# The first half tile of a fused attention-memory and MoE kernel as a fixed script with plain 32-bit products

## The chip, the cores and the metric

The kernel runs on one core of one Trainium2 chip. The metric is the device time of one execution in microseconds (us). TensorE (PE) does the matrix products, VectorE (DVE) and ScalarE (ACT) the work on elements, GpSimd (POOL) and SyncE (SP) mostly issue transfers (DMA).

## What is computed

Four batches of eight heads with 576 tokens each go through an attention on a small memory; its output, 2304 tokens of 512, goes through two layers with 2048 hidden features.

```python
a = exp(phi - max(phi, axis=2)); a = a / (sum(a, axis=2) + 1e-9)     # 4 x 8 x 576 x 32, over the tokens
k_m = einsum('bhsm,bhsd->bhmd', a, k); v_m = einsum('bhsm,bhsd->bhmd', a, v)
scores = q @ k_m.T / sqrt(64)                                        # 576 x 32 for each head
attn = softmax(scores)                                               # over the 32 memory rows
x = attn @ v_m                                                       # 2304 x 512
x = square(relu(x @ w_in1)) @ w_out1                                 # layer 1
h = x @ w_in2; x = (h * tanh(softplus(h))) @ w_out2                  # layer 2
```

The weights arrive as 64-bit floats, which the kernel reads as pairs of 32-bit words and turns into 32-bit floats itself.

## The kernel before

**Tiles.** Layer 1 works on half tiles (b, half) of T = 288 tokens. The features are taken in groups of 4, 6 and 6 chunks of 128 (`GROUPS`); for each group the loop over `subs` runs through (0,0), (0,1), (1,0) and (1,1), and batches 2 and 3 follow later. The attention's last product is not made on its own: `w_part` (L474) and `w_turn` (L488) multiply v_m with W_in1 into `wp`, and a chunk's `h` is `wp` times the attention weights `a_t`. `a_tile` (L567) does one half tile: for each chunk six products for `h` (L580 to L582), relu (L589), square (L590), a high part `g` on ACT (L594) and the low part on DVE (L597); three chunks later (LAG = 3) `mm2_step` (L536) adds twelve products into four accumulators `a` (L542 to L544). Each product of two 32-bit matrices is written as three products of high and low parts (high by high, low by high, high by low).

**Weights.** `Conv` (L147), called c1, loads raw weights of 512 KB and converts 32 of them for layer 1: a Prelu on ACT (L185), a shift (L207) and a shift with "or" (L214) on DVE, and for W_out1 a high cast on ACT (L180) and a low part on DVE (L222). Each chunk calls `tick` (L168) once, and `c1.limit` says up to which conversion it may start. `win` are the converted pages of W_in1, which L218 also writes back to memory (`w_i`) for later use; `ct_o` and `o1h`, `o1l` are those of W_out1. A raw buffer that comes free lets SP issue the next load (L164).

**Attention.** For batch b `kv_soft` (L349) takes the maximum and exponential of phi, `kv_turn` (L359) transposes them (`pt`, `et`), `kv_mem` (L382) makes k_m and v_m (`pk`, `kk`), `kv_heads` (L405) turns those into `kT` and `vT` by way of `pkt`. `attn_unit` (L433) computes the scores of one half tile (`psc`, L439), their softmax on DVE and ACT, the transposed weights `at` (L462), and their high and low parts `ah` (L468) and `al` (L469). It is a generator in four steps; the lists `lanes` hand such steps out, one or three for each chunk.

**Order.** The pools and the tile framework decide the order of the instructions on an engine by their data and by `behind(...)`, which makes an instruction wait for a mark; `ahead` (L346) places products of h behind pieces of batch 1's memory and scores. Eight products of the identity with itself (`warm`, L629) run ahead of everything. All loads go through one queue on SP; they land in the order of issue.

## Time and profile before

| | us |
|---|---|
| median of 3 runs | 753.77 (751.84 to 756.18) |
| the profiled execution | 753.87 |
| its span on the core | 752.1 |
| PE busy | 722.5 |
| DVE busy | 527.0 |
| ACT busy | 420.3 |

The page counts for each engine the time in which it executed something; a share is an average over stretches with different limits. An idle time stands with the instruction that follows it, with the engine that released that instruction. The granted clock of PE is either full (1.00) or half (0.50).

### The profile page before, as it was taken

The numbers are of one execution on the slowest core, as the hardware profiler recorded it, in microseconds if no ns is written. First come the engines' busy times: TensorE is split into PE (matmuls) and PEld (weight loads), VectorE is DVE, ScalarE is ACT, GpSimd is POOL, SyncE is SP. The second block draws the span as 40 slices with busy tenths as digits, with TensorE's granted clock in tenths as the row PEclk, the third lists the DMA queues.
The fourth block names the chain that finished last, engine by engine and source line by source line (L and its number), as shares of the span: only waits on it lengthen the run. The fifth ranks groups of instructions, "written<-read, shape, count | busy, mean of one in ns | idle before, by whom it ended". The sixth has DMA issues, their size and how long they took to land.

```text
span 752.1 us, 16243 instructions
## 1 busy us (share of the span) xinstructions
PE 722.5 (96%) x5984; PEld 695.1 (92%) x5984; DVE 527.0 (70%) x1129; ACT 420.3 (56%) x960; POOL 62.3 (8%) x120
## 2 busy tenths in 40 slices
PE   5699999999998999989999999999999999999998
PEld 4487899999887989889999999999999999999998
...
PEclk9699999999999999999999999999999999999999
...
GB/s 334 405 407 73 202 189 144 182 240 359 316 338 273 172 249 305 266 280 261 343 39 322 259 267 352 244 302 263 323 267 255 248 285 278 256 236 270 245 266 73
DMA packets 89327, 195.33 MB, mean 260 GB/s; under 512 B 9888, under 2 KB 22688, under 8 KB 89248
## 3 DMA queue, kind: packets, MB, share of 16 engines
...
q10 hardware_dynamic: 144, 0.13, 0.1%
...
## 4 chain that ended last, share of the span: by engine, by line
PE 77%; DMA 6%; issue 6%; ACT 5%; DVE 3%; POOL 2%; SPq 0%; POOLq 0%; ACTq 0%
PE hb L979 8%; PE hb L981 8%; PE hb L980 8%; PE a L542 6%; PE a L544 6%; PE a L543 6%; PE h L580 3%; PE h L582 3%; PE h L581 3%; DMA raw_i<-in_moe_w_in_dram 2%; POOL wf_o L302 2%; DMA kv<-in_kvm_dram 1%; DMA wf_o<-st 1%; PE pk L397 1%; DMA wf_i<-st 1%
## 5 line engine op out<-in xcount | busy, mean ns | idle before, releaser
L542 PE MATMUL a<-g,o1h 128*128 128x288 f32 x512 | 147.9, 299 | 3.8 <-DVE g L596 1.1
L543 PE MATMUL a<-g,o1l 128*128 128x288 f32 x512 | 147.1, 297 | 0.0
L544 PE MATMUL a<-g,o1h 128*128 128x288 f32 x512 | 127.0, 296 | 0.8 <-DVE g L597 0.5
L979 PE MATMUL hb<-ych,u 128*128 128x384 f32 x336 | 112.9, 336 | 0.1
L980 PE MATMUL hb<-ycl,u 128*128 128x384 f32 x336 | 113.0, 336 | 0.0
L1024 DVE TENSOR_TENSOR opl<-a,oph 128x384 fp32r<-128x384 f32 x144 | 79.1, 557 | 46.9 <-ACT oph L1023 46.3
L981 PE MATMUL hb<-ych,u 128*128 128x384 f32 x336 | 109.5, 336 | 0.0
L1023 ACT CAST oph<-a 128x384 fp32r<-128x384 f32 x144 | 73.9, 513 | 58.8 <-PE b20b L1047 7.0
L542 PEld LDWEIGHTS a<-g,o1h 128*128 128x128 f32 x512 | 96.3, 189 | 7.0 <-ACT g L594 2.8
L543 PEld LDWEIGHTS a<-g,o1l 128*128 128x128 f32 x512 | 96.6, 189 | 0.0
L985 ACT ACTIVATE a<-hs 128x384 f32<-128x384 f32 x72 | 37.8, 525 | 98.1 <-DVE hs L989 98.0
L544 PEld LDWEIGHTS a<-g,o1h 128*128 128x128 f32 x512 | 88.5, 190 | 2.7 <-DVE g L597 1.9
L580 PE MATMUL h<-ah,wp 128*128 128x288 f32 x256 | 79.2, 311 | 6.8 <-ACT wp L485 2.7
L589 ACT ACTIVATE s<-h 128x288 f32<-128x288 f32 x128 | 52.3, 410 | 56.1 <-PE h L582 53.9
L582 PE MATMUL h<-ah,wp 128*128 128x288 f32 x256 | 76.4, 300 | 0.7 <-DVE wp L486 0.7
L581 PE MATMUL h<-al,wp 128*128 128x288 f32 x256 | 76.4, 299 | 0.0
L597 DVE TENSOR_TENSOR g<-s,g 128x288 fp32r<-128x288 f32 x128 | 57.0, 451 | 17.9 <-ACT g L594 16.8
L989 DVE TENSOR_TENSOR hs<-hu,hb 128x384 f32<-128x384 f32 x72 | 39.8, 554 | 40.7 <-PE hb L981 40.1
L979 PEld LDWEIGHTS hb<-ych,u 128*128 128x128 f32 x336 | 63.0, 188 | 0.4 <-DMA u<-wf_i 0.4
L980 PEld LDWEIGHTS hb<-ycl,u 128*128 128x128 f32 x336 | 63.0, 188 | 0.0
L981 PEld LDWEIGHTS hb<-ych,u 128*128 128x128 f32 x336 | 62.8, 188 | 0.0
L580 PEld LDWEIGHTS h<-ah,wp 128*128 128x128 f32 x256 | 48.5, 190 | 15.4 <-ACT wp L485 3.6
...
## 6 DMA issues: line engine op xcount, KB each, us to landing
u<-wf_i SPq DMA_DIRECT2D x168, 256.0 KB, 3.7
u<-wf_o SPq DMA_DIRECT2D x168, 256.0 KB, 3.4
raw_i<-in_moe_w_in_dram SPq DMA_DIRECT2D x32, 512.0 KB, 6.1
raw_o<-in_moe_w_out_dram SPq DMA_DIRECT2D x32, 512.0 KB, 6.0
wf_o<-st POOLq DMA_DIRECT2D x56, 256.0 KB, 4.9
wf_i<-st POOLq DMA_DIRECT2D x44, 256.0 KB, 4.5
win1r<-w_i SPq DMA_DIRECT2D x16, 512.0 KB, 6.8
...
```

The source lines that it names most:

```text
L542: nc.tensor.matmul(o, wh[:, c, cs], sh, start=first, stop=False)
L543: nc.tensor.matmul(o, wl[:, c, cs], sh, start=False, stop=False)
L544: done_pe["main"] = nc.tensor.matmul(o, wh[:, c, cs], sl, start=False, stop=last)
L580: nc.tensor.matmul(ph, w[:, 0, hg, fs], hi[:, hg], start=(hg == 0), stop=False)
L581: nc.tensor.matmul(ph, w[:, 0, hg, fs], lo[:, hg], start=False, stop=False)
L582: done_pe["h"] = nc.tensor.matmul(ph, w[:, 1, hg, fs], hi[:, hg], start=False, stop=(hg == 1))
L597: marks["low"] = nc.vector.tensor_sub(sl, s, sh.bitcast(F32))
L979: nc.tensor.matmul(ps, wh, yh[:, d], start=(j < 4 and d == 0), stop=False, **kw)
L980: nc.tensor.matmul(ps, wh, yl[:, d], start=False, stop=False, **kw)
L981: nc.tensor.matmul(ps, wl, yh[:, d], start=False, stop=end, **kw)
L1023: marks["s"] = nc.scalar.copy(hi, x)
L1024: marks["v"] = sub(lo, x, hi.bitcast(F32))
```

## The change

Engines are wrapped in a class `Engine`; while `strict` is on, each engine's instructions are issued in the order in which they are written. The beginning up to the end of the first four chunks of tile (0,0) is written out as such a script. These four chunks are 24 plain products of 32-bit operands, eight for h and sixteen for a, in the place of 72 products of high and low parts; the high and low parts of `wp`, of `a_t` of tile (0,0) and of W_out1 are made afterwards. 27 more products of the identity are strewn among PE's instructions. `kk` (its part for v) and `vT` of batch 0 go to ACT. The loads have another order: the tail of k and v and raw_i_0 stand ahead of q, batch 1's loads behind the reads of batch 0's buffers. The converted pages `w_i` are written back from POOL's queue. `c1.limit` for tile (0,1) is 8 in the place of 11. The attention of (0,1) lies in the script; the memory and scores of batch 1 begin in tile (0,1). Everywhere else `nc.tensor`, `nc.scalar`, `nc.vector` and `nc.sync` become `pe`, `act`, `vec` and `sp`.

```diff
+class Engine:
+
+
+    def __init__(self, tc, engine):
+        self.tc, self.engine, self.strict, self.last = tc, engine, False, None
+
+    def __getattr__(self, name):
+        f = getattr(self.engine, name)
+        if not self.strict or (name == "dma_start" and self.engine is not self.tc.nc.sync):
+            return f
+
+        def issue(*args, **kw):
+            if self.last is None:
+                self.last = f(*args, **kw)
+            else:
+                with self.tc.issue_after(self.last.ins):
+                    self.last = f(*args, **kw)
+            return self.last
+        return issue
...
     def load_first(i):
+        sp.dma_start(tails[:, i].rearrange("p g d -> p (g d)"), kvt[0, i])
         for p in range(2):
-            nc.sync.dma_start(kv_t[0, p][i].rearrange("p g c d -> p (g c d)"), kvm[0, p, i])
-        nc.sync.dma_start(tails[:, i].rearrange("p g d -> p (g d)"), kvt[0, i])
+            sp.dma_start(kv_t[0, p][i].rearrange("p g c d -> p (g c d)"), kvm[0, p, i])
 
     load_first(0)
-    load_q(0, 0)
...
+        def begin(self):
+            key, u = self.order[self.started]
+            high = self.raw[key, u][:, :, 1].bitcast(F32)
+            with behind(marks, "step" if self.paced else None):
+                act.activation(high, high, AF.Prelu, scale=2.0 ** -112, alpha=-2.0 ** 32)
+            self.started += 1
+            return [key, u, 0, None, None]
...
-                    nc.sync.dma_start(w1[x[1] // 2], wt["i1", x[1] // 2])
...
+                nc.gpsimd.dma_start(w1[u // 2], wt["i1", u // 2])
+            self.raw.pop((key, u))
+            if not self.hold:
+                self.load()
...
-    ahead = {(0, 0, 3): ("pt", 1, 0), (0, 1, 0): ("pk", 1, 0), (0, 1, 1): ("pk", 1, 1),
-             (0, 1, 2): ("pkt", 1), (0, 1, 3): ("psc", 1, 0)}
+    ahead = {(0, 1, 0): "first"}
...
-            nc.vector.tensor_copy(vT[b], ps[:, P:2 * P])
...
+            (act.copy if b == 0 else vec.tensor_copy)(vT[b], ps[:, P:2 * P])
...
-    c1.limit = 2 * GROUPS[0]
+    strict(True)
...
     c1.load(1)
+    load_q(0, 0)
     load_first(1)
-    c1.load(2)
+    c1.load(4)
     load_q(0, 1)
-    c1.load(6)
-    warm = bank("acc3", "warm")
-    for _ in range(N_WARM):
-        nc.tensor.matmul(warm[:, :P], ident, ident, start=True, stop=True)
-
+    c1.load(3)
+    warm = bank("b0", "warm")
+    def warm_up(n):
+        for _ in range(n):
+            pe.matmul(warm[:, :P], ident, ident, start=True, stop=True)
+    warm_up(N_WARM)
     kv_soft(0, 0)
     kv_soft(0, 1)
     kv_turn(0, 0, ("acc0", "acc1"))
     kv_turn(0, 1, ("acc2", "acc3"))
+    load_phi(1, 0)
+    load_phi(1, 1)
+    warm_up(6)
     kv_mem(0, 0, (0,), "acc0")
     kv_mem(0, 1, (0,), "acc1")
+    warm_up(2)
     kv_heads(0, (0,), "acc2")
-    at00 = attn_unit(0, 0, lambda: load_q(1, 0))
+    conv = [c1.begin()]
+    c1.hold = True
+    c1.bits(conv[0])
+    warm_up(3)
+    at00 = attn_unit(0, 0, fine=True)
     next(at00)
-    c1.after = (0, 0)
-    c1.tick()
+    warm_up(6)
+    kv_mem(0, 0, (1,), "acc3")
+    warm_up(4)
     next(at00)
-    kv_mem(0, 0, (1,), "acc3")
+    next(at00)
     kv_mem(0, 1, (1,), "acc0")
-    c1.tick()
+    warm_up(2)
     kv_heads(0, (1,), "acc1")
-    next(at00)
-    w_part(0, 0, 0, P)
-    next(at00)
-    c1.tick()
-    c1.after = (0, 0)
-    load_phi(1, 0)
-    load_phi(1, 1)
     load_kv(1, 0)
     load_tail(1)
     kv_t[1, 1] = tuple(page([P, 4, NC, D], F32, f"kv11{i}") for i in "kv")
     for i in range(2):
-        nc.sync.dma_start(kv_t[1, 1][i].rearrange("p g c d -> p (g c d)"), kvm[1, 1, i])
+        sp.dma_start(kv_t[1, 1][i].rearrange("p g c d -> p (g c d)"), kvm[1, 1, i])
+    load_q(1, 0)
+    c1.hold = False
+    c1.load(2)
+    conv.append(c1.begin())
+    next(at00)
+    next(at00)
+    plain = page([P, 2, 2, 256], F32, "plain")
+    plain = [plain[:, i] for i in range(2)]
+    ps = banks2("pw000")[:, :, :P]
+    w_mm(ps, 0, 0, 0, P)
+    act.copy(plain[0][:, :, :P], ps)
+    warm_up(4)
+    a32 = a_t[0]
+    n_first = GROUPS[0]
+    hs = {}
+    def first_h(fc):
+        hs[fc] = bank("mm", f"h00_{fc}")[:, :T]
+        for hg in range(2):
+            pe.matmul(
+                hs[fc], plain[fc // 2][:, hg, (fc % 2) * P:(fc % 2) * P + P], a32[:, hg],
+                start=(hg == 0), stop=(hg == 1))
+    def relu(fc):
+        s = X.tile([P, 2, T], F32, tag="g", name=f"s00_{fc}", bufs=4)[:, 0]
+        marks["step"] = act.activation(s, hs[fc], AF.Relu)
+        hs[fc] = s
+    def square(fc):
+        act.activation(hs[fc], hs[fc], AF.Square)
+    acc00 = [bank(f"acc{d}", f"a00{d}") for d in range(4)]
+    done00 = evac_y1(0, 0, True, False)
+    def first_a(fc):
+        for dm in range(4):
+            o = acc00[dm][:, :T]
+            done_pe["first"] = pe.matmul(
+                o, conv[n_first + fc][3][:, dm * P:dm * P + P], hs[fc],
+                start=(fc == 0), stop=(fc == n_first - 1))
+    def place(i):
+        t = Y.tile([P, 2, T], F32, tag=f"ys{2 + i % 2}", name=f"ct0{i}", bufs=2)
+        return t.rearrange("p a t -> p (a t)")[:, :512]
+    def begin(n=1):
+        conv.extend(c1.begin() for _ in range(n))
+    begin(2)
+    for x in conv[1:4]:
+        c1.bits(x)
+    first_h(0)
+    relu(0)
+    ps = banks2("pw001")[:, :, :P]
+    w_mm(ps, 0, 0, P, 2 * P)
+    act.copy(plain[0][:, :, P:], ps)
+    square(0)
+    begin()
+    c1.bits(conv[4], place(0))
+    first_h(1)
+    relu(1)
+    square(1)
+    ps = banks2("pw01")[:, :, :256]
+    w_mm(ps, 0, 1)
+    act.copy(plain[1], ps)
+    begin()
+    c1.bits(conv[5], place(1))
+    at01 = attn_unit(0, 1, lambda: load_q(1, 1), fine=True)
+    next(at01)
+    next(at01)
+    next(at00)
+    first_h(2)
+    relu(2)
+    square(2)
+    begin()
+    first_h(3)
+    relu(3)
+    next(at01)
+    square(3)
+    begin()
+    for i in range(2):
+        w_high(0, i, plain[i])
+    next(at01)
+    c1.bits(conv[6], place(2))
+    next(at01)
+    c1.high(conv[4])
+    c1.bits(conv[7], place(3))
+    next(at01)
+    for i in range(2):
+        w_low(0, i, plain[i])
+    for fc in range(n_first):
+        first_a(fc)
+    for x in conv[5:]:
+        c1.high(x)
+    for i, x in enumerate(conv[4:]):
+        if i < 2:
+            kv_soft(1, i)
+        c1.low(x)
+        if i == 1:
+            for dm in range(4):
+                done00(dm, acc00[dm][:, :T])
+    c1.done |= {(x[0], x[1]) for x in conv}
+    strict(False)
+    marks["step"], marks["first"], done_pe["main"] = act.last, vec.last, done_pe["first"]
...
-            u = lazy(lambda: attn_unit(0, 1, lambda: load_q(1, 1)))
-            lanes = [[u, 1], [soft_both(1), 1], [u, 3]] + kv_later(1) + attn_later(1, 0)
-            n_steps = 3
-        elif i == 1:
-            assert (0, 1) in a_t
-            c1.limit, c1.after, c1.paced = 2 * GROUPS[0] + 3, (0, 1), True
-            n_steps = 1
+            continue
+        if i == 1:
+            c1.limit, c1.after, c1.paced = 2 * GROUPS[0], "first", True
+            lanes, n_steps = [[iter(range(3)), 3]] + kv_later(1) + attn_later(1, 0), 3
```

In the script `fine=True` splits `attn_unit` into six steps, `w_mm`, `w_high` and `w_low` are the three parts of `w_part`, and `bits`, `high` and `low` are the parts of a conversion that `tick` did before.

PE at the scores of batch 1's first half tile, before: `psc` are scores, `a` and `h` the products of tile (0,1), and the last number of a name is only a count.

```order
L439 MATMUL psc_591<-q_229,kT_587 32x288 x4
L439 MATMUL psc_591<-q_231,kT_587 32x288 x4
L544 MATMUL a_625<-g_0_640,o1h_394 128x288
L544 MATMUL a_626<-g_0_640,o1h_394 128x288
L544 MATMUL a_627<-g_0_640,o1h_394 128x288
L544 MATMUL a_628<-g_0_640,o1h_394 128x288
L580 MATMUL h_2_697<-ah_448,wp_419 128x288
L581 MATMUL h_2_697<-al_449,wp_419 128x288
L582 MATMUL h_2_697<-ah_448,wp_419 128x288
```

The same place now; `pw10p` is `w_turn`, the second `psc` the scores of tile (1,1), and `h_0` the first chunk of tile (1,0).

```order
L576 MATMUL a_522<-g_3_710,o1h_500 128x288
L576 MATMUL a_523<-g_3_710,o1h_500 128x288
L576 MATMUL a_524<-g_3_710,o1h_500 128x288
L576 MATMUL a_525<-g_3_710,o1h_500 128x288
L472 MATMUL psc_659<-q_319,kT_655 32x288 x4
L472 MATMUL psc_659<-q_321,kT_655 32x288 x4
L515 MATMUL pw10p<-win_0_229,vT_657 32x256 x8
L515 MATMUL pw10p<-win_1_361,vT_657 32x256 x8
L472 MATMUL psc_787<-q_424,kT_655 32x288 x4
L472 MATMUL psc_787<-q_426,kT_655 32x288 x4
L612 MATMUL h_0_742<-ah_722,wp_694 128x288
L612 MATMUL h_1_768<-ah_722,wp_694 128x288
```

Before, three products of a and the chunks h_2 and h_3 of tile (0,1) stood behind these scores; now the last products of that tile stand ahead of them, and tile (1,0) follows behind w_turn and the other scores.

ACT at the beginning, before: `kT` scales k_m for the scores, raw_i are the Prelu operations of the weight conversions, `et` the transposed exponentials.

```order
L378 COPY et_149<-pt_150 128x512
L378 COPY et_161<-pt_162 128x512
L185 ACTIVATE raw_i_0_105<-raw_i_0_105 128x512
L413 ACTIVATE kT_218<-pkt_216 128x128
L185 ACTIVATE raw_i_1_110<-raw_i_1_110 128x512
L453 ACTIVATE x_233<-x_233 128x576
L185 ACTIVATE raw_o_0_112<-raw_o_0_112 128x512
L185 ACTIVATE raw_i_2_118<-raw_i_2_118 128x512
L468 CAST ah_314<-at_312 128x576
L485 CAST wp_309<-pw_300 128x2x128
```

The same place now; L53 is the line of the wrapper, `plain` holds a 32-bit `wp`.

```order
L53 COPY et_147<-pt_148 128x512
L53 COPY et_159<-pt_160 128x512
L53 ACTIVATE kT_226<-pkt_224 128x128
L53 ACTIVATE raw_i_0_101<-raw_i_0_101 128x512
L53 ACTIVATE kk_198<-pk_255,rc_139 128x64
L53 ACTIVATE x_244<-x_244 128x576
L53 ACTIVATE kk_198<-pk_283,rc_143 128x64
L53 COPY vT_309<-pkt_307 128x128
L53 ACTIVATE raw_i_1_110<-raw_i_1_110 128x512
L53 COPY plain<-pw_336 128x2x128
```

kT now stands ahead of the first raw_i, the v part of kk and vT have come to ACT, and the high parts ah and wp are gone from here.

DVE behind `al` of tile (0,1), before: L207 and L214 (`win_2`, `ct_o_4`) are conversions, `g` the low parts of tile (0,1).

```order
L469 TENSOR_TENSOR al_449<-at_446,ah_448 128x576
L207 TENSOR_SCALAR win_2_668<-raw_i_4_128 128x4x128
L207 TENSOR_SCALAR win_2_668<-raw_i_5_289 128x4x128
L207 TENSOR_SCALAR ct_o_4_764<-raw_o_4_322 128x512
L214 SCALAR_TENSOR_TENSOR win_2_668<-raw_i_4_128,win_2_668 128x4x128
L597 TENSOR_TENSOR g_3_581<-s_3_580,g_3_581 128x288
L402 TENSOR_SCALAR kk_504<-pk_517,rc_390 128x2x64
L561 COPY ys_719<-a_346 128x288
L214 SCALAR_TENSOR_TENSOR win_2_668<-raw_i_5_289,win_2_668 128x4x128
L561 COPY ys_728<-a_348 128x288
L597 TENSOR_TENSOR g_0_640<-s_0_639,g_0_640 128x288
L416 COPY vT_589<-pkt_584 128x128
```

DVE behind `at` of tile (1,0), now: the same two conversions of raw_i, and raw_o_4.

```order
L497 STREAM_TRANSPOSE at_720<-x_672 128x576
L507 TENSOR_TENSOR al_723<-at_720,ah_722 128x576
L213 TENSOR_SCALAR win_2_776<-raw_i_4_323 128x4x128
L213 TENSOR_SCALAR win_2_776<-raw_i_5_325 128x4x128
L213 TENSOR_SCALAR ct_o_4_860<-raw_o_4_359 128x512
L481 STREAM_TRANSPOSE x_796<-psc_787 128x288 x2
L215 SCALAR_TENSOR_TENSOR win_2_776<-raw_i_4_323,win_2_776 128x4x128
L483 TENSOR_REDUCE smx_799<-x_796 128x18
L485 TENSOR_TENSOR x_796<-x_796,smx_799 128x576
L215 SCALAR_TENSOR_TENSOR win_2_776<-raw_i_5_325,win_2_776 128x4x128
L215 SCALAR_TENSOR_TENSOR ct_o_4_860<-raw_o_4_359,ct_o_4_860 128x512
L629 TENSOR_TENSOR g_0_753<-s_0_752,g_0_753 128x288
```

The conversions of raw_i_4, raw_i_5 and raw_o_4 stood between the low parts of tile (0,1); now they stand beside the first chunks of tile (1,0).

## Rows read from the trace of the kernel before

**Rows 1.** The page, sections 1 and 2: PE busy; granted clock by slices.
```profile
PE 722.5 (96%) x5984; PEld 695.1 (92%) x5984; DVE 527.0 (70%) x1129; ACT 420.3 (56%) x960; POOL 62.3 (8%) x120
...
PEclk9699999999999999999999999999999999999999
```

**Rows 2.** Stretches by engine: length, busy (count) of each, clock, DMA, GB/s.
```profile
core 0: us, PE busy (x) PEld busy (x) DVE busy (x) ACT busy (x) POOL busy (x), PEclk, DMA share, GB/s
...
20.00:33.00 13.00, 9.16 (x70) 6.23 (x71) 12.11 (x27) 8.52 (x18) 0.00 (x0) 0.50 1.04 402
...
60.00:80.00 20.00, 18.14 (x149) 15.99 (x148) 18.99 (x43) 16.97 (x42) 0.00 (x0) 1.00 0.21 79
80.00:100.00 20.00, 20.00 (x176) 19.30 (x175) 16.97 (x35) 16.85 (x42) 0.00 (x0) 1.00 0.62 201
```

**Rows 3.** Timeline 10 to 23 us: start, duration, line, operation [idle before <-releaser].
```profile
12.33 0.65 ACT L185 ACTIVATE raw_i<-raw_i 128x512 f32<-128x512 f32 x1 [4.99 <-DMA raw_i<-in_moe_w_in_dram]
...
13.19 1.22 PE L439 MATMUL psc<-q,kT 64*32 64x288 f32 x16 [1.87 <-ACT kT L413]
...
14.54 0.85 DVE L448 STREAM_TRANSPOSE x<-psc 128x288 f32<-128x288 f32 x2 [3.59 <-PE psc L439]
...
20.27 0.77 DVE L462 STREAM_TRANSPOSE at<-x 128x576 f32<-128x576 f32 x1
...
22.22 0.61 PE L580 MATMUL h<-ah,wp 128*128 128x288 f32 x1 [1.14 <-ACT wp L485]
```

**Rows 4.** ACT's timeline: the Prelu that waits for raw_o_1.
```profile
23.23 0.67 ACT L185 ACTIVATE raw_o<-raw_o 128x512 f32<-128x512 f32 x1 [0.50 <-DMA raw_o<-in_moe_w_out_dram]
```

**Rows 5.** PE's timeline: h(0,1), the scores of (1,0), h(1,0).
```profile
44.45 0.40 PE L580 MATMUL h<-ah,wp 128*128 128x288 f32 x1
44.69 0.29 PE L581 MATMUL h<-al,wp 128*128 128x288 f32 x1
44.82 0.29 PE L582 MATMUL h<-ah,wp 128*128 128x288 f32 x1
...
49.11 0.72 PE L439 MATMUL psc<-q,kT 64*32 64x288 f32 x16
...
57.59 0.53 PE L580 MATMUL h<-ah,wp 128*128 128x288 f32 x2 [1.04 <-ACT ah L468]
```

**Rows 6.** Groups by form, 0 to 80 us: count, busy us, mean ns, idle.
```profile
L214 DVE SCALAR_TENSOR_TENSOR win<-raw_i,win 128x512 int32<-128x512 int32 x10 | 6.7, 685 | 0.0
...
L222 DVE TENSOR_TENSOR o1l<-ct_o,o1h 128x512 fp32r<-128x512 f32 x7 | 4.8, 689 | 0.3 <-ACT o1h L180 0.3
...
L207 DVE TENSOR_SCALAR win<-raw_i 128x512 int32<-128x512 int32 x11 | 4.3, 422 | 0.0
...
L629 PE MATMUL warm<-ident 128*128 128x128 f32 x16 | 3.8, 431 | 1.5 <-POOL ident masks.py:199 1.5
...
L450 DVE TENSOR_REDUCE smx<-x 128x18 f32<-128x576 f32 x4 | 3.0, 750 | 0.1
```

**Rows 7.** Timelines of DVE and ACT: the ends of the chain to h(1,0).
```profile
50.32 0.84 DVE L448 STREAM_TRANSPOSE x<-psc 128x288 f32<-128x288 f32 x2
...
56.86 0.67 ACT L468 CAST ah<-at 128x576 fp32r<-128x576 f32 x1
```

**Rows 8.** SP's waits up to 60 us, and its issue of a raw load.
```profile
SPq L164 <- DVE win L214: 9.3, 1, 9.3
...
61.73 0.33 SPq L164 DMA_DIRECT2D raw_i<-in_moe_w_in_dram  x1
```

**Rows 9.** Stretches around a pause of PE, columns as in rows 2.
```profile
237.00:240.00 3.00, 0.63 (x7) 0.43 (x6) 1.50 (x4) 1.08 (x4) 0.54 (x1) 1.00 1.00 404
...
241.20:244.60 3.40, 3.40 (x27) 2.70 (x27) 1.05 (x3) 1.48 (x4) 0.32 (x1) 0.51 0.49 195
```

**Rows 10.** The page, section 6: DMA issues: KB each, median us to landing.
```profile
raw_i<-in_moe_w_in_dram SPq DMA_DIRECT2D x32, 512.0 KB, 6.1
...
wf_o<-st POOLq DMA_DIRECT2D x56, 256.0 KB, 4.9
```

More of the change, by code (lines that the diff above doesn't have):

```diff
@@ L173, in tick @@
             for x in ends:
[L174 to L187 removed]
+                self.high(x)
+            if start and self.started < min(self.loaded, self.limit) and self.ready(*self.order[self.started]):
+                self.flight.append(self.begin())
             with behind(marks, self.after):
[L189 removed]
+                for x in bits:
+                    self.bits(x)
+                for x in ends:
+                    self.low(x)
             for x in self.flight:
@@ L609, in body @@
     for f0, f1 in zip(bounds, bounds[1:]):
+        if f0 == 0:
+            order += [(key, f) for key in ("i1", "o1") for f in range(f1)]
+            continue
         order += [("i1", f0), ("i1", f0 + 1)]
@@ L1091, in b_step @@
             if j == 4:
-                each(nc.scalar.copy, t)
+                each(act.copy, t)
             else:
```

266 lines of the change are left out of this document (126 added, 140 removed).

## The prediction

> **What bounds the kernel now.** I read the page first: TensorE (PE) is busy for 722.5 of the 752.1 us [rows 1], so the time goes down only where PE stands still, and the change touches only the first 80 us or so. The stretches come next [rows 2]: from 20 to 33 us PE is busy for 9.16 of 13.00 us at a granted clock of 0.50, while VectorE (DVE) is busy for 12.11: there PE waits for DVE. From 60 to 80 us PE stands for 1.86 us and DVE is busy for 18.99 of 20. From 80 us on PE has no gap (20.00 of 20.00), and DVE 3.0 us of room. So the beginning has to be followed instruction by instruction up to about 80 us; a lead or a lag that PE has there is kept to the end, since no gap follows that could take it up. Three places do that: the first scores and the first h of tile (0,0) [rows 3], the load that arrives last for it [rows 4], and PE's h(0,1), scores of batch 1 and h(1,0) [rows 5].
>
> **The change up to h(0,1).** Loads land in the order in which they are issued. The second half of q now has the place that raw_i_0 had before, and that landed at 12.33 (the Prelu had waited 4.99 us for it) [rows 3]. kT now stands ahead of that Prelu on ACT, so the scores wait only for q: 12.3 and 0.65 for 8 score products at full clock give DVE's first transposes at 13.1 instead of 14.54, a gain of 1.4. The DVE row from there is 0.85, 3 passes over x of 0.75 [rows 6], 0.67 for the exponential on ACT, 0.17, 0.27, 0.76 and 0.77, in all 5.8: the attention of (0,0) stands at 18.9, and h can begin at 19.0 instead of 22.22, since the plain products need neither the high cast on ACT nor the low part on DVE.
>
> Then DVE has three weight conversions of 0.42 + 0.69 = 1.11 [rows 6], to 22.2, and ct of raw_o_0, to 23.3. The next one needs raw_o_1. That load has the same 7104 KiB ahead of it in both kernels, so it lands at 23.2 as before [rows 4]; a Prelu of 0.68 and the 0.69 of the second shift give 24.6. What follows on DVE up to the low parts of tile (0,1) is fixed by the script: transposes 0.84, maximum 0.75, difference 0.75, low of (0,0) 0.76, sum, EPS, reciprocal and product 1.95, two conversions 2.22, transpose 0.77, low of (0,1) 0.76 and two lows of wp 1.38, in all 10.2. This ends at 34.8. PE is there at the same time: the last four a products follow the last ct at 32.6 with 4 times 0.5. So **h(0,1) begins at about 34.7 instead of 44.45** [rows 5], 9.7 us earlier.
>
> What a plain product costs: eight warm-ups of 128 columns take 3.78 us (two records for each) at a granted clock of 0.5, 0.47 each [rows 6]; 288 columns are then 1.06, and 0.53 at full clock, an estimate from that row. The 24 plain products are 12.7 us at full clock against 72 times 0.13 [rows 5] = 9.6 for the products that they replace. That dearer work costs nothing as long as DVE's row, up to 34.8, covers it, and it is covered at full clock only. The 27 added warm-ups, 27 times 0.24 = 6.4 us at full clock, lie where PE waits for DVE and the loads; they are there at nothing, with up to 0.5 if one delays a score product.
>
> Edits at nothing: kk and vT of batch 0 go from DVE to ACT (three of about 0.28, ACT is busy for 8.52 of 13.00 [rows 2]); batch 1's kv, q and raw loads stay in one queue on SyncE behind batch 0's reads, and what waits for them, batch 1's memory products, comes only at 39.7 in my row, while the reads of batch 0 end near 17; w_i leaves SP's queue for POOL's, so that raw loads no longer stand behind it. 256 KB written from POOL's queue land after 4.9 us [rows 10], and nobody waits for w_i's landing before its buffer is used again tens of us later.
>
> Whether the clock stays full from 19 to 33 decides 4 us (first rival). The row of before has 0.50 there, with PE busy for only 9.16 of 13.00 us [rows 2]. The changed row of PE has warm-ups, products and plain products from 1.5 us on with few pauses, so I take full clock. The Trainium skill, "TensorE: Matmul & The Clock Gate", section "Part 1: The HAM clock gate (the "warmup" mystery)", says that the throttled state is the default and that activity releases it. The trace agrees with its first half in the 0.50 beside 3.84 us without work, and shows no stretch of 32-bit products alone at full clock. By that rule the sum would stay at +3.0, by the row of before it would be +7.0.
>
> **Where the lead goes.** In the changed kernel batch 1's softmax, memory products and scores start only in tile (0,1). DVE's maxima end at 36.9 (34.8 and 0.75, a low of 0.69, 0.75), then ACT has the exponential (0.96), two copies of a (0.82) and et (0.69): et is there at 39.4, with the hand-overs 39.7. From there PE's row has no gap: pk and pt 1.7, h_2 and h_3 1.6, 48 a products 6.4, the other pk and pkt 1.5, in all 11.2. The scores of (1,0) begin at **50.9; before they began at 49.11** [rows 5]. The 9.7 us have become a lag of 1.8.
>
> Behind these scores comes a chain that is the same in both: scores, softmax on DVE and ACT, ah, h(1,0). It took from 49.11 to 57.59, 8.48 us [rows 5], with DVE from 50.32 and ah at 56.86 [rows 7]; and PE stood for only 1.04 of it, because h_2, h_3 and a_0 to a_2 of tile (0,1), left over, filled it. In the changed order only w_turn and the scores of (1,1) stand between: 0.7 + 1.1 + 0.7 = 2.5 us of work. PE will stand for about 6 us, and h(1,0) begins at 50.9 + 8.5 = 59.4. In exchange nothing of tile (0,1) is left to do, where before had a_3 (1.6) and the scores of (1,1) (0.7) still to come at 57.59: it was level at 59.9. **Net −0.5.** Bounds: −1.9 with the bare chain (7.1: the operations alone, without the g casts and low parts between them), +0.5 if pk finds et 1 us later.
>
> **Three conversions come later.** raw_i_4, raw_i_5 and raw_o_4 were converted in tile (0,1) and are now held for tile (1,0): on DVE 3 times 1.11 and one low of 0.69, 4.0 us, in the stretch where DVE had 20 − 18.99 = 1.0 of room [rows 2]. **+3.0**; bounds 0 (DVE's order lets PE's work pass) and +4.0 (no room).
>
> **The clock after the pause.** PE pauses for 2.37 us between 237 and 240; from 241.2 to 244.6 the granted clock is 0.51 [rows 9]: 3.4 us at half, 1.7 lost. The new pause of 6 us before h(1,0) may have the same behind it, in a stretch where PE partly waits anyway: **+0.5**, bounds 0 and +1.7.
>
> Sum: −0.5 + 3.0 + 0.5 = **+3.0**. The profiled execution took 753.87 (span 752.1), 0.1 above the median of the runs; on the median 753.77 + 3.0 = 756.8. The likeliest case's own range: 753.9 (bare chain, half of the conversions' cost: −1.9 + 1.5 + 0.5) to 758.8 (+0.5 + 4.0 + 0.5).
>
> **Rivals.** *The clock falls in the plain products (slower).* Before, it was 0.50 from 20 to 33 [rows 2]; if the strewn warm-ups and the plain products don't hold it up, the 8 h products and the pw and scores end near 30 instead of before 27, three of 16 a products are through at 33, and 13 times 0.53 = 6.9 gives h(0,1) at 39.9. On ACT et stands behind the relu of that h: relu 0.41, square 0.45, exponential 0.96, copies 0.82, et 0.69 put it at 43.9, 4 later. 756.8 + 4 = 760.8. At 4 for 13 us, 2.5 us at half clock already bring the sum past 0.5%. For it: the row of before. Against it: PE now has work nearly without a pause from 1.5 us on.
>
> *A late raw load (slower).* Before, SyncE waited 9.3 us for a raw buffer until DVE's L214 was through, and issued raw_i at 61.73 [rows 8]. With the conversions held back, that buffer comes free some 12 us later, near 74, and by the page's median of raw_i, 6.1 [rows 10], it lands at 80. If its place on ACT and DVE is at 76, both stand for up to 4 us, of which DVE's room in 80 to 100 takes 3.0 only in part: +2, 758.8. For it: that wait. Against: much of the third group is needed late.
>
> *Chain and conversions both fit (faster).* DVE's row in 60 to 80 was long because of the work that before did there late; with the chain bare (−1.9), conversions that fit, no fall of the clock, and before's own idle of PE (1.04 ahead of h(1,0) [rows 5], 1.86 in 60 to 80 [rows 2]) not coming back: −4.8, 749.0.
>
> *The change does nothing for the time.* The script saves 9.7 us up to h(0,1), the order behind it gives all back, and the conversions fit: 753.8.
>
> **How the numbers follow.** Forecast 0.48; of it 0.30 within 0.5% (3.77 us, about what a measurement of this kernel can tell from no change: 750.0 to 757.5) and 0.18 above. Clock 0.14, slower. Late load 0.13 (0.10 slower, 0.03 same). Everything fits 0.17 (0.14 faster, 0.03 same). Nothing 0.08, same. Faster 0.14, same 0.44, slower 0.42. The range from 749.5 to 762.0 leaves out about 0.10 below (the better half of the case that fits) and 0.06 above (the clock case with the upper bounds).
>
> **What would show it.** Right: transposes of (0,0) at 13.1, first h at 19, h(0,1) at 34 to 36, scores of (1,0) at 50 to 52, a PE gap of 5 to 7 us before h(1,0) near 59.4, and DVE without a gap up to 75 with PE standing for 3 us more than before in 60 to 80. Wrong: a granted clock of 0.5 in 20 to 33 (first rival); ACT waiting for raw_i's load between 70 and 85 (second); PE at 19.5 or more in 60 to 80 (third); or scores of (1,0) before 48, which would say that I misread what et or the memory products wait for.

## The result and the profile after

The changed kernel is slower. Its median is 760.42 us (756.56 to 762.96) against 752.9 for the kernel before in the same comparison. The ratio on record is 1.0074 (95% interval 1.0047 to 1.0101); it is estimated over all runs and is not the quotient of the two medians, which is 1.0100. A second comparison (e13 below) gave 1.0058 (1.0035 to 1.0082; medians 757.95 and 754.46), so the loss is some 4.4 to 5.6 us, about 0.6 to 0.7%. Of the 19 executions of the changed kernel in both comparisons 12 took 756.0 to 758.3 us and 7 took 760.4 to 763.2, none between, and the two traces are of the first kind. The prediction was 756.8 in a range of 749.5 to 762.0, with the chances nearly even between "within 0.5%" and slower. The profiled execution took 757.44 us, with a span of 755.6.

The page of the changed kernel, busy time of the engines and the granted clock in 40 slices:

```profile
PE 730.8 (97%) x6014; PEld 701.3 (93%) x6014; DVE 525.8 (70%) x1121; ACT 420.0 (56%) x961; POOL 67.0 (9%) x128
...
PEclk9998999999999999999999999999999999999999
```

PE is busy 8.3 us more than before [rows 1] in a span that is 3.5 us longer. The forecast's estimates for the 27 warm-ups (6.4 us) and for the dearer plain products (3.1) are together of that size.

Its stretches by engine (busy time and count of PE, PEld, DVE, ACT, POOL; then clock, DMA share, GB/s):

```profile
20.00:33.00 13.00, 10.72 (x83) 6.81 (x83) 11.26 (x22) 9.86 (x21) 1.22 (x2) 1.00 1.03 409
...
57.00:60.00 3.00, 1.56 (x17) 0.61 (x18) 2.26 (x4) 0.72 (x2) 0.00 (x0) 0.50 0.02 5
60.00:80.00 20.00, 19.47 (x148) 16.74 (x147) 19.41 (x44) 15.26 (x39) 1.07 (x2) 0.94 0.46 158
80.00:100.00 20.00, 19.98 (x173) 19.16 (x173) 16.07 (x34) 17.52 (x44) 1.07 (x2) 1.00 0.43 141
```

Against [rows 2]: the clock is full from 20 to 33 us, where it was half; it is half from 57 to 60; and PE is busy for 19.47 us of 60 to 80, where it was 18.14.

PE's timeline in the changed kernel: the first scores, the first h, h(0,1), the scores of (1,0), w_turn, the scores of (1,1) and h(1,0):

```profile
11.71 0.71 PE L53 MATMUL psc<-q,kT 64*32 64x288 f32 x16
...
18.93 1.14 PE L53 MATMUL h<-at,plain 128*128 128x288 f32 x4
...
35.35 0.51 PE L612 MATMUL h<-ah,wp 128*128 128x288 f32 x1
...
51.05 0.71 PE L472 MATMUL psc<-q,kT 64*32 64x288 f32 x16
52.90 1.10 PE L515 MATMUL pw10p<-win,vT 64*32 64x256 f32 x32 [1.13 <-DVE x L481]
58.31 1.21 PE L472 MATMUL psc<-q,kT 64*32 64x288 f32 x16 [4.31 <-issue]
59.65 0.85 PE L612 MATMUL h<-ah,wp 128*128 128x288 f32 x2
```

These rows answer to [rows 3, 5]. The first scores begin at 11.71 instead of 13.19, the first h at 18.93 instead of 22.22, h(0,1) at 35.35 instead of 44.45, nine us ahead. The scores of (1,0) are at 51.05 (before 49.11), PE then stands for 1.13 and 4.31 us, and h(1,0) is at 59.65 (before 57.59). For the 4.31 us the profile names no releaser ("issue"); the second scores begin just after DVE has made the second low part of wp. What h(1,0) waits for last is the high part of the attention weights on ACT:

```profile
58.93 0.67 ACT L506 CAST ah<-at 128x576 fp32r<-128x576 f32 x1 [1.88 <-DVE at L497]
```

**How the rest is followed.** From h(1,0) on both kernels have the same products to do. I take a product of the kernel before at some time, count the products behind it in its trace, and look for the product of the other kernel that has as many behind it. The difference of the two starts is the lag of the other kernel. Where the order of small pieces differs it is off by some tenths; a few records are missing in a trace.

| us in before | 60 | 62 | 85 | 100 | 115 | 122 | 320 | 340 | 700 | ratio of times (95%) |
|---|---|---|---|---|---|---|---|---|---|---|
| changed | -0.46 | 0.99 | -0.03 | 0.06 | 0.64 | 3.30 | 1.30 | 3.15 | 3.55 | 1.0074 (1.0047 to 1.0101) |
| e13, the same again | -0.81 | 0.95 | -0.34 | -0.25 | 1.15 | 2.52 | 1.25 | 3.32 | 3.51 | 1.0058 (1.0035 to 1.0082) |
| e1, limit 11 | 6.21 | 7.63 | 7.36 | 7.43 | 7.42 | 8.65 | 6.88 | 9.34 | 9.66 | 1.0096 (1.0067 to 1.0125) |
| e2, warm-ups in the pause | -0.36 | 0.37 | 0.70 | 1.24 | 2.03 | 4.03 | 3.31 | 6.89 | 7.73 | 1.0073 (1.0048 to 1.0097) |
| e3, eight warm-ups only | 5.62 | 7.41 | 7.62 | 7.67 | 8.47 | 9.13 | 7.06 | 7.19 | 7.55 | 1.0087 (1.0061 to 1.0113) |
| e4, before with limit 8 | 0.67 | 0.67 | -0.14 | 0.43 | 0.42 | 1.54 | 2.11 | 1.38 | 1.45 | 1.0001 (0.9976 to 1.0026) |
| e5, early kv | 0.16 | 2.00 | 2.16 | 2.21 | 2.21 | 4.26 | 2.05 | 4.48 | 4.88 | 1.0057 (1.0028 to 1.0087) |
| e7, w_i on SP | -0.25 | 1.12 | 0.26 | 0.29 | 1.58 | 1.93 | 1.44 | 1.59 | 1.93 | 1.0062 (1.0034 to 1.0089) |
| e8, kv before h_2 | -2.46 | -2.20 | -1.49 | -0.17 | -0.11 | 1.35 | -0.70 | 2.97 | 3.35 | 1.0031 (1.0008 to 1.0054) |
| e9, the same with limit 11 from chunk 1 | -2.86 | -2.60 | -0.25 | -0.19 | -0.17 | 0.50 | -0.92 | 1.08 | 1.41 | 1.0012 (0.9990 to 1.0033) |
| e10, e9 with short conversions | -1.73 | -1.45 | -0.55 | -0.53 | -0.50 | -0.51 | -3.19 | -0.35 | -0.18 | 1.0003 (0.9985 to 1.0020) |
| e11, changed with short conversions | -0.35 | 1.73 | 0.32 | 0.43 | 1.93 | 6.18 | 3.35 | 5.93 | 6.83 | 1.0073 (1.0047 to 1.0099) |
| e12, more conversions early | -1.11 | -0.08 | 1.64 | 2.57 | 7.18 | 7.98 | 6.65 | 8.37 | 8.70 | 1.0083 (1.0053 to 1.0114) |

So the lead of nine us at h(0,1) is half a us at 60, and a lag of one at 62, where the clock is half; that is earned back by 85; from 100 to 122 come 3 us. This last place, in the changed kernel, PE and then DVE:

```profile
121.36 0.40 PE L574 MATMUL a<-g,o1h 128*128 128x288 f32 x1 [2.36 <-DVE ys L589]
```

```profile
120.51 0.43 DVE L213 TENSOR_SCALAR ct_o<-raw_o 128x512 int32<-128x512 int32 x1 [2.55 <-DMA raw_o<-in_moe_w_out_dram]
120.85 0.81 DVE L589 TENSOR_TENSOR ys<-a,ys 128x288 f32<-128x288 f32 x2
```

PE waits 2.36 us for a sum of y1 on DVE, and DVE had stood for 2.55 us, with that sum queued behind it, for a raw load.

These 3 us do not simply stay. At 310 us the lag is still 3.37, at 320 it is 1.30 and at 340 again 3.15. First the kernel before and then the changed one, columns as above:

```profile
310.00:325.00 15.00, 13.53 (x100) 13.00 (x99) 14.54 (x42) 8.94 (x26) 8.51 (x15) 1.00 0.95 333
332.00:335.40 3.40, 3.40 (x28) 3.40 (x28) 2.77 (x9) 1.74 (x6) 1.61 (x3) 1.00 0.67 246
```

```profile
310.00:325.00 15.00, 15.00 (x115) 15.00 (x114) 15.00 (x43) 10.25 (x29) 8.62 (x14) 1.00 0.94 317
332.00:335.40 3.40, 3.26 (x13) 3.26 (x14) 3.40 (x12) 2.30 (x8) 1.96 (x4) 0.50 0.61 237
```

From 310 to 325 us PE of the kernel before stands for 1.5 us and the changed one's does not, and the lag falls by 2 us. Near 330 both pause (before 0.82 and 1.11 us, changed 0.95 and 1.27), and then the clock of the changed kernel is half for 3.4 us, while before it stays full: that takes the 2 us again. Ten of the fourteen traces here have this half clock (it begins between 329.8 and 338.6 us), and lose 1.7 to 3.7 us from 320 to 340; e3 and e7 do not have it and lose 0.1 and 0.2, and of the two versions of the old order neither has it. So what a trace shows at 700 us also depends on this place.

### The profile page after: what moved, and what is told of

It reads as the page before. It is cut to its first block, busy times and chain, and to the rows that moved or that the text cites. A ratio compares the mean times of both kernels' runs of the same rounds, so it can differ in the third digit from the quotient of the medians.

```text
span 755.6 us, 16307 instructions
## 1 busy us (share of the span) xinstructions
PE 730.8 (97%) x6014; PEld 701.3 (93%) x6014; DVE 525.8 (70%) x1121; ACT 420.0 (56%) x961; POOL 67.0 (9%) x128
## 4 chain that ended last, share of the span: by engine, by line
PE 77%; DMA 9%; issue 5%; DVE 4%; ACT 3%; POOL 2%; POOLq 0%; DVEq 0%; ACTq 0%
PE hb L1109 8%; PE hb L1110 8%; PE hb L1111 8%; PE a L576 6%; PE a L574 6%; PE a L575 6%; PE h L612 3%; PE h L613 3%; PE h L614 3%; DMA kv<-in_kvm_dram 2%; DMA raw_i<-in_moe_w_in_dram 2%; DMA raw_o<-in_moe_w_out_dram 2%; POOL wf_o L333 2%; PE warm L53 1%; DMA wf_o<-st 1%
## 5 line engine op out<-in xcount | busy, mean ns | idle before, releaser
L574 PE MATMUL a<-g,o1h 128*128 128x288 f32 x496 | 144.3, 300 | 4.5 <-DVE ys L589 2.9
L575 PE MATMUL a<-g,o1l 128*128 128x288 f32 x496 | 142.8, 296 | 0.0
L576 PE MATMUL a<-g,o1h 128*128 128x288 f32 x496 | 125.6, 298 | 0.2 <-DVE g L629 0.2
L574 PEld LDWEIGHTS a<-g,o1h 128*128 128x128 f32 x496 | 93.7, 189 | 7.5 <-DVE ys L589 3.6
L575 PEld LDWEIGHTS a<-g,o1l 128*128 128x128 f32 x496 | 93.9, 189 | 0.0
L576 PEld LDWEIGHTS a<-g,o1h 128*128 128x128 f32 x496 | 86.3, 189 | 1.2 <-DVE g L629 0.9
L621 ACT ACTIVATE s<-h 128x288 f32<-128x288 f32 x124 | 50.7, 410 | 57.0 <-PE h L614 55.8
L612 PE MATMUL h<-ah,wp 128*128 128x288 f32 x248 | 76.7, 311 | 2.6 <-ACT s L621 2.4
L613 PE MATMUL h<-al,wp 128*128 128x288 f32 x248 | 74.0, 299 | 0.0
L614 PE MATMUL h<-ah,wp 128*128 128x288 f32 x248 | 73.7, 299 | 0.0
L629 DVE TENSOR_TENSOR g<-s,g 128x288 fp32r<-128x288 f32 x124 | 55.4, 452 | 21.1 <-ACT g L626 20.7
```

What stands on the lines that cost most here:

```text
L574: pe.matmul(o, wh[:, c, cs], sh, start=first, stop=False)
L575: pe.matmul(o, wl[:, c, cs], sh, start=False, stop=False)
L576: done_pe["main"] = pe.matmul(o, wh[:, c, cs], sl, start=False, stop=last)
L612: pe.matmul(ph, w[:, 0, hg, fs], hi[:, hg], start=(hg == 0), stop=False)
L613: pe.matmul(ph, w[:, 0, hg, fs], lo[:, hg], start=False, stop=False)
L614: done_pe["h"] = pe.matmul(ph, w[:, 1, hg, fs], hi[:, hg], start=False, stop=(hg == 1))
```

## The experiments

**e1: the limit back at 11.** In the planning of tile (0,1):

```diff
-            c1.limit, c1.after, c1.paced = 2 * GROUPS[0], "first", True
+            c1.limit, c1.after, c1.paced = 2 * GROUPS[0] + 3, "first", True
```

> The changed kernel with the limit for tile (0,1) back at 11, so that raw_i_4, raw_i_5 and raw_o_4 are converted in that tile again. Theory (the holding back of three conversions makes a raw load late, and DVE stands for it at 118 to 120.5 us with the y1 sums and PE behind it): the 2.4 us pause of PE near 119 is gone, PE's lag against before at 136 us falls from +3.3 to +1 or less, and the time is 2 to 3 us under the changed kernel's, near 0 to 1 against before. Rival (the lag comes from the order of loads in the script, not from the limit): the pause stays, 0 to 0.5 us gained. Second rival (the conversions push tile (0,1)): h(1,0) begins 1 to 3 us later and eats the gain.

The second rival held, and at more than it said: ratio 1.0096. ACT and PE in e1:

```profile
40.76 0.67 ACT L197 ACTIVATE raw_i<-raw_i 128x512 f32<-128x512 f32 x1 [2.96 <-DMA raw_i<-in_moe_w_in_dram]
...
43.54 0.69 ACT L406 COPY et<-pt 128x640 f32<-128x640 f32 x1
```

```profile
44.28 1.93 PE L427 MATMUL pk<-kv,et 128*32 128x128 f32 x32 [5.17 <-ACT et L406]
```

In this load order raw_i_4 lands only at 40.7. Its Prelu on ACT waits for it with the exponential of phi, the y1 copies and et in line behind, and PE waits 5.17 us for et. The limit of 8 keeps a late load out of ACT's line at this place. The lag grows by 1.23 from 115 to 122 us, against 2.66 in the changed kernel and 1.37 in its second trace (e13): the pause near 119 does not go away with the old limit, and whether it is smaller this pair does not show.

**e2: warm-ups in the pause ahead of h(1,0).**

```diff
+            ahead[1, 0, 0] = "gap"
+            warm2 = bank("b0", "warm2")
+            for _ in range(18):
+                with behind(done_pe, "turn"):
+                    done_pe["gap"] = pe.matmul(warm2[:, :P], ident, ident, start=True, stop=True)
```

("turn" is the last product of w_turn.)

> The changed kernel with 18 products of the identity between w_turn and the scores of (1,1), in the pause before h(1,0). Theory (the pause lets the clock fall, and the half clock after it costs 1.45 us, from -0.46 to +0.99 of lag): granted clock 1.00 from 57 to 62, lag after the first h products near -0.5, but the lag at 136 us only as far lower as the late load at 119 allows, 0 to 1.4 us. Rival (the clock's cost is hidden behind DVE, which converts in that stretch): lag at 70 us as in the changed kernel, no gain.

Stretches of e2:

```profile
57.00:60.00 3.00, 2.28 (x29) 1.58 (x29) 2.26 (x4) 0.83 (x2) 0.00 (x0) 1.00 0.00 0
60.00:62.50 2.50, 2.23 (x16) 1.93 (x16) 2.50 (x7) 0.98 (x3) 0.00 (x0) 1.00 0.00 0
```

The clock is full there, and the lag at 62 us is 0.37 instead of 0.99: the half clock costs 0.6 us up to there. Taking it away brings nothing: at 85 us e2 lags by 0.70, the kernel without it by -0.03, and the ratio is the same. The rival held: what the half clock takes after this pause, later waits have room for.

**e3: without the 27 strewn warm-ups.** Each `warm_up(n)` behind the first, `warm_up(N_WARM)`, is removed.

> The changed kernel without the 27 strewn products of the identity, the first eight alone. Forecast's theory (they hold the clock): without them the granted clock is 0.5 in part of 7 to 33 us, h(0,1) begins at 37 to 40 instead of 35.35, time +2 to +4 us against the changed kernel. Rival (the plain products and the pw hold it by themselves): clock 1.00 from 20 to 33, time within 0.5 us of the changed kernel.

One stretch of e3:

```profile
20.00:33.00 13.00, 11.22 (x65) 5.33 (x64) 7.51 (x14) 6.05 (x13) 1.21 (x2) 0.50 1.03 409
```

The clock is half from 17.9 to 35.0 us (in the changed kernel it is full from 7.7 to 55.5), h(0,1) begins at 41.48 instead of 35.35, and the lag at 85 us is 7.62 instead of 0. The 24 plain products and the small pw products alone don't hold the clock here. In time it is less: 1.0087 against 1.0074 and 1.0058, with overlapping intervals. In the traces the difference shrinks from 7.7 us at 85 to 4.0 at 700, since e3 has a pause of only 0.4 us at the late raw load and no half clock near 330; how many of the 7 us come back in most runs isn't settled.

**e4: the kernel before with the limit at 8.**

```diff
-            c1.limit, c1.after, c1.paced = 2 * GROUPS[0] + 3, (0, 1), True
+            c1.limit, c1.after, c1.paced = 2 * GROUPS[0], (0, 1), True
```

> The kernel before with only the limit for tile (0,1) lowered from 11 to 8: the holding back alone. Theory (late load): a pause of PE for a raw load near 110 to 120 us, time +2 to +3.5 us against before. Rival (the holding back matters only with the script's other order of loads): within 0.7 us of before. If the conversions cost PE on DVE as the forecast's term said, PE lags 2 to 3 us already at 80 us.

The time is that of before (1.0001). The trace has the mechanism in small. DVE in e4, and the same wait of the kernel before:

```profile
118.75 0.43 DVE L207 TENSOR_SCALAR ct_o<-raw_o 128x512 int32<-128x512 int32 x1 [2.02 <-DMA raw_o<-in_moe_w_out_dram]
```

```profile
117.21 0.43 DVE L207 TENSOR_SCALAR ct_o<-raw_o 128x512 int32<-128x512 int32 x1 [1.60 <-DMA raw_o<-in_moe_w_out_dram]
```

Before, DVE already waits 1.60 us for this raw load, and nobody on PE notices; held back by 1.5 us it costs PE a pause of 0.86. So the theory that the holding back alone makes the loss fell. And with the three conversions held PE is level at 85 us (-0.14), where the forecast's term had 3 us of lag.

**e5: batch 1's softmax ahead of the low parts of wp, no empty steps.**

```diff
+    kv_soft(1, 0)
+    kv_soft(1, 1)
     for i in range(2):
         w_low(0, i, plain[i])
...
-        if i < 2:
-            kv_soft(1, i)
...
-            lanes, n_steps = [[iter(range(3)), 3]] + kv_later(1) + attn_later(1, 0), 3
+            lanes, n_steps = kv_later(1) + attn_later(1, 0), 3
```

> The changed kernel with batch 1's two softmax steps on DVE and ACT moved ahead of the low parts of wp at the end of the script, and without the three empty steps ahead of batch 1's memory. Theory (the lead up to h(0,1) is lost because the scores of (1,0) come last in tile (0,1), and nothing is left to cover their chain): scores of (1,0) at 48 to 49 instead of 51.05, a_3 of tile (0,1) behind them, h(1,0) at 56.5 to 57.5 instead of 59.65, lag at 62 us -1 to -2 instead of +1, and 1.5 to 3 us less time if nothing else bounds there. Rival (DVE's conversions bound the stretch from 60 to 100 us, whatever PE's lead): PE waits later and the lag at 100 us is 0 as in the changed kernel.

It missed: the scores of (1,0) are at 51.07, no earlier. et comes 0.7 us sooner, but PE then pauses for 1.96 us instead of 1.15, its clock is half from 40 to 42, and the planner still puts 36 of the 48 a products ahead of the scores. Ratio 1.0057, within the error of the changed kernel's.

**e7: w_i written from SP's queue.**

```diff
-                nc.gpsimd.dma_start(w1[u // 2], wt["i1", u // 2])
+                sp.dma_start(w1[u // 2], wt["i1", u // 2])
```

> The changed kernel with the write-back of w_i on SyncE's queue again. Theory (the pause at 119 us comes from raw loads whose buffers are given back late, not from the queue): pause near 119 stays at 1 to 2.5 us, time within 1 us of the changed kernel. Rival (POOL's writes collide with the raw load or land late while DVE works): pause gone, 2 us less. Second rival (on SyncE the raw loads stand behind the writes): 1 us more.

Of the theory the time held (1.0062, that of the changed kernel), the pause did not: DVE waits for the raw load at 119.1 for 0.84 us, and PE behind it hardly stands (its lag grows by 0.35 from 115 to 122). The loss from 100 to 122 us is 1.64 instead of 3.24 and 2.77. But at 300 us the lag is 3.48 as in the changed kernel (3.34), since PE waits 3.75 us for a load of kv ahead of 243.7 where that one waits 2.11; only the full clock near 330 makes the 1.93 at the end. The queue may have a part; one trace and this interval don't show it.

**e8: chunk 2 of tile (0,1) behind the scores of (1,0).** e5, and

```diff
-    ahead = {(0, 1, 0): "first"}
+    ahead = {(0, 1, 0): "first", (0, 1, 2): ("psc", 1, 0)}
```

> As e5_early_kv, and chunk 2 of tile (0,1) is held behind the scores of (1,0) on PE. Theory of the uncovered chain: scores of (1,0) at 42 to 44, with h_2, h_3, w_turn and 24 a products (about 6 us) over their chain, h(1,0) at 51 to 54 instead of 59.65, PE's lag at 62 us -4 to -6. What is then the bound decides the time: if DVE's conversions (held for tile (1,0)) are, the lag shrinks to -1 to 0 at 100 us; if not, 4 to 6 us less time than the changed kernel.

PE in e8, the scores of (1,0) and h(1,0):

```profile
48.60 0.72 PE L472 MATMUL psc<-q,kT 64*32 64x288 f32 x16 [0.37 <-ACT kT L446]
...
57.66 0.43 PE L612 MATMUL h<-ah,wp 128*128 128x288 f32 x2
```

The scores are 2.5 us earlier, with h_2, h_3, w_turn and two chunks of a over their chain, and PE's 4.3 us pause is gone; the lag at 60 us is -2.46 instead of -0.46. The direction held, not the size: the scores are at 48.6, not 43, and the lag at 62 us is -2.20, not -4 to -6. The wait just ahead of the scores is for kT on ACT, the last of kk, pkt and kT, which follow one another on DVE, PE and ACT; besides, the clock is half from 39.7 to 43.1. What each takes of the 5 us was not measured. At 100 us the lead is gone (-0.17), as expected if something bounds that stretch. Ratio 1.0031.

**e9: e8 with the conversions from chunk 1 on.**

```diff
         def tick(fc):
+            if i == 1 and fc == 1:
+                c1.limit = 2 * GROUPS[0] + 3
```

> As e8_kv_before_h2, with the limit raised to 11 from chunk 1 of tile (0,1) on, so that the held conversions begin where DVE stood (41 to 50 us in the changed kernel). Theory (conversions bound after the chain is covered): lag at 100 us 1.5 to 3 us lower than in e8, pause at 119 gone, time 3 to 6 us under the changed kernel, level with or under before. Rival (as in e1_limit11 the conversions push DVE's part of batch 1's memory): scores of (1,0) 1 to 3 us later than in e8, no gain over it.

Of its theory the time held (1.0012: 0.5 to 0.6% under the changed kernel, level with before), the rest not: the lag at 100 us is that of e8, and a pause near 119 is still there, smaller (0.38 us of PE). PE's waits of e9 where its 2.9 us of lead go:

```profile
63.83 0.79 PE L576 MATMUL a<-g,o1h 128*128 128x288 f32 x4 [1.41 <-DVE g L629]
...
70.40 0.53 PE L612 MATMUL h<-ah,wp 128*128 128x288 f32 x2 [0.96 <-ACT ah L506]
...
71.19 0.40 PE L613 MATMUL h<-al,wp 128*128 128x288 f32 x1 [0.27 <-DVE al L507]
...
78.80 0.40 PE L612 MATMUL h<-ah,wp 128*128 128x288 f32 x1 [1.04 <-ACT wp L521]
```

1.41 for a low part g on DVE, 0.96 and 0.27 for the high and low part of (1,1)'s attention, 1.04 for wp on ACT. Before, PE had 0.40, 0.31, 0.18 and 0.71 there in all.

**e10: e9 with ten short conversions.** For raw_i_4 to raw_i_9 and raw_o_4 to raw_o_7 the low word is left out:

```diff
+            if (key, u) in (("i1", 4), ("i1", 5), ("i1", 6), ("i1", 7), ("i1", 8), ("i1", 9), ("o1", 4), ("o1", 5), ("o1", 6), ("o1", 7)):
+                vec.tensor_scalar(
+                    out=d, in0=self.word(x, 1), scalar1=3, scalar2=None, op0=ALU.logical_shift_left)
+            else:
```

> As e9_kv_before_h2_limit, and ten conversions (raw_i_4 to raw_i_9, raw_o_4 to raw_o_7) leave out the low word: one shift on DVE (about 0.4 to 0.7 us) in the place of 1.11 us. Theory (PE's lead at 60 us is lost because DVE bounds 60 to 80 us): DVE has some 4 to 6 us less to do there, and the lag at 80 to 100 us stays at -2 to -4 instead of -0.25; time 2 to 3 us under e9. Rival (something else makes the floor at 80 us: ACT, or the landing of raw loads): the lag comes back to -0.3 at 80 to 100 us.

PE's waits in the same stretch:

```profile
63.83 0.79 PE L580 MATMUL a<-g,o1h 128*128 128x288 f32 x4 [0.29 <-DVE g L633]
...
70.95 0.40 PE L617 MATMUL h<-al,wp 128*128 128x288 f32 x1 [1.05 <-DVE al L511]
...
78.21 0.40 PE L616 MATMUL h<-ah,wp 128*128 128x288 f32 x1 [1.17 <-ACT wp L525]
```

The first wait shrinks from 1.41 to 0.29, but only because PE comes 1.1 us later: these products begin at 63.83 in both. The product that waits for the low part of (1,1)'s attention begins at 70.95 instead of 71.19, the one behind wp at 78.21 instead of 78.80. So shorter conversions move these places by 0, 0.2 and 0.6 us, and the theory that they bound the stretch from 60 to 80 fell: the lag at 85 is -0.55. The softmax of (1,1) and w_turn, which pass through DVE and ACT, are what PE waits for there; which step of them is the bound was not tested. The pause at 119 us is gone altogether (lag -0.50 at 115, -0.51 at 122).

**e11: the changed kernel with the same short conversions.** The diff is that of e10.

> The changed kernel with the same ten conversions shortened (low word left out). Theory (the changed kernel has no lead at 60 us that DVE could take away, only the loss of clock that it earns back by 80 us): lag at 85 to 100 us -1 to -2.5 instead of 0, since DVE is relieved there too, and the rest of the lag at 119 us as in the changed kernel; time 1 to 2.5 us under it. Rival (DVE is no bound for it): lag at 85 to 100 us within 0.4 of 0.

The rival held, within a tenth: 0.32 at 85 us, 0.43 at 100, and 1.0073. The pair is not clean, since the half clock after the first pause lasts from 54.9 to 65.1 us in this trace. The pause at 119 is there unchanged (PE 2.45 us), and the clock falls behind it.

**e12: two conversions in each chunk of (0,1).** e9 with a limit of 14 and

```diff
+            if i == 1 and fc >= 1:
+                c1.tick()
```

> As e9_kv_before_h2_limit, with two conversions started in each chunk of tile (0,1) from chunk 1 on (limit 14), whole ones. Theory (DVE stands in 41 to 50 us and bounds 60 to 80 us): moving about three more conversions into the earlier stretch gives a lag of -2 to -3.5 at 80 to 100 us, and 1 to 3 us less time than e9, under the kernel before. Rival (they push batch 1's memory and scores as in e1_limit11): scores of (1,0) 1.5 to 3 us later than in e9, no gain or a loss.

The rival held, at its lower end: the scores of (1,0) are at 49.32 instead of 47.92, the lag at 85 us is 1.64, and one raw load is late earlier. DVE in e12:

```profile
107.28 0.43 DVE L213 TENSOR_SCALAR ct_o<-raw_o 128x512 int32<-128x512 int32 x1 [2.79 <-DMA raw_o<-in_moe_w_out_dram]
```

PE pauses for 2.81 us there, the clock is half from 108.9 to 112.3, and the lag jumps from 2.57 to 7.18. Starting conversions sooner did not bring the raw loads sooner in this trace.

**e13: the changed kernel once more.**

> The changed kernel once more, for a second trace of it. Theory (half clock after the pause, then a raw load that DVE waits for near 119 us): lag -0.5 at 60 us, +0.7 to +1.8 at 62, 0 to 0.5 at 85 to 105, a pause of 1.5 to 3 us between 114 and 122 us and +3 to +6 at 136, as in the first trace and in e11. Rival (the pause near 119 was an accident of the first trace): lag at 136 us under +1.5, and the extra time elsewhere.

The theory held in kind, and its sizes near 119 us did not: the lags at 60 to 100 us are those of the first trace within 0.4, the clock is half from 55.8 to 62.7, DVE waits 1.12 us for the raw load at 119.7 and PE behind it for 1.07 (forecast 1.5 to 3), the lag is 2.52 at 122 us (forecast +3 to +6 at 136) and 3.5 at the end. Here 0.9 of the loss come already at 103 us, where PE waits 0.66 for another sum of y1.

**What makes the raw load late.** The chain of waits of the changed kernel from 100 to 125 us (start, duration):

```profile
101.46 4.82 DMA raw_o<-in_moe_w_out_dram
...
106.29 0.71 ACT raw_o L197
...
107.02 0.70 DVE ct_o L215
...
107.75 4.62 DMA raw_o<-in_moe_w_out_dram
...
114.04 6.38 DMA raw_o<-in_moe_w_out_dram
...
120.51 0.43 DVE ct_o L213
120.94 0.38 DVE ys L589
```

It is a ring: a buffer is loaded (4.8 us, 4.6, 6.4), converted, and only then gives its place to the load of a later page. SP's issues of the last pair of raw_o of the group, in before and in the changed kernel:

```profile
109.21 1.95 SPq L164 DMA_DIRECT2D raw_o<-in_moe_w_out_dram  x2
```

```profile
112.22 2.14 SPq L189 DMA_DIRECT2D raw_o<-in_moe_w_out_dram  x2
```

3.0 us later, with PE at 109 us at a lag of 0.4. Why the ring is 3 us behind PE there, I could not pin on one part: the held conversions (holding them alone brings 1.1 us from 115 to 122 in e4, releasing them takes 0.8 away from e8 to e9, and e1 has as much as e13), w_i's queue (e7, not beyond its error) and DVE's load (e10 removes the pause, e11 doesn't) each touch it. A fourth raw buffer would test the ring itself; it wasn't tried, so that the ring is the cause is argued from the chain and not shown.

## Why the prediction was right, and where it was not

**Up to h(0,1).** Right: the first h at 18.93 (19.0), h(0,1) at 35.35 (34.7). The first scores came at 11.71, 0.6 us sooner than the place of q in the queue had said, with DVE's transposes at 12.63 (13.1). What that gained was gone at raw_o_1: DVE waits 0.72 us for its Prelu, which stands behind the copy of `plain` on ACT and not behind the load, and is through at 24.86 (24.6). Two readings of the forecast are off without effect: the 7104 KiB include raw_o_1 itself (6592 lie ahead of it), and in 20 to 33 us PE of the kernel before waits more for ACT's casts of wp (2.7 us) than for DVE (1.7).

**Where the lead goes.** Right in mechanism and size: scores of (1,0) at 51.05 (50.9), 1.13 and 4.31 us of pause (6), h(1,0) at 59.65 (59.4), net -0.46 (-0.5). e8 shows the cause: with work left over their chain the scores, which also begin 2.5 us sooner there, no longer leave PE standing for 4.3 us, and 2 us come out at 60.

**The clock in the plain products.** The first rival did not come, since the warm-ups hold the clock; e3 shows that it would have without them, with h(0,1) at 41.48 where the rival's working said 39.9. The Trainium skill, "TensorE: Matmul & The Clock Gate", section "Part 1: The HAM clock gate (the "warmup" mystery)", says that the throttled state is the default and that activity releases it. This pair agrees: 0.50 from 20 to 33 us without the strewn products, 1.00 with them.

**Three conversions, +3.0: wrong.** The lag went from 0.99 at 62 to -0.03 at 85, so the term was -1.0, outside its lower end of 0; e4, with the same three conversions held in the old order, is at -0.14 there. I had taken DVE's 1.0 us of room in [rows 2] as the room that PE had. But before, PE itself stood in that stretch for 1.86 us, of which the changed order needed only 0.5 (19.47 of 20). The third rival's argument, that before's own pauses need not come back, was the right one here, and I had put it into the faster case alone; its sign, PE at 19.5 or more in 60 to 80, was met but for 0.03.

**The clock after the pause, +0.5: right in size.** The lag went from -0.46 to 0.99, by 1.45, but in e2, with the clock full, it goes from -0.36 to 0.37: 0.6 to 0.7 of it are the clock's. The rest of the step I had not foreseen; it may lie in the different order of small pieces at 60 us. It did not add to the sum: with the last term it was earned back by 85 us.

**The late raw load.** The second rival had the mechanism (a buffer that DVE gives back late, a load that lands late, DVE in order behind it), priced at +2 and placed at raw_i between 70 and 85 us. It came 40 us later, at raw_o, for +2.66 and +1.37 between 115 and 122 us. This and not the conversions' work on DVE is what makes the lag of 3.3 and 2.5 at 122.

**Nothing behind 80 us can take up a lag: wrong.** The forecast kept every lead or lag of 80 us to the end, since no gap follows. But from 310 to 325 us PE of the kernel before stands for 1.5 us, and both traces of the changed kernel get about 2 us back there; and the half clock near 332 takes 1.9 and 2.1 again, which no term had.

**The sum.** +3.0 forecast, +3.5 in both traces, out of other terms. In the first trace they are -0.46 at 60 us, +1.45 to 62, -1.0 to 85, +3.3 to 122, -2.0 to 320, +1.9 to 340 and 0.4 behind it, where I had -0.5, +0.5, +3.0 and nothing. Up to h(1,0) the forecast was right for its reasons; that the sum fits is luck. The ratios say 4.4 to 5.6 us, 1 to 2 more than the traces. Where those are, the traces of the changed kernel do not show; that of e2, at 761.6 us, loses 3.6 from 320 to 340, so the place near 330 can cost that much. It stays open.
